# Attention and gated layer in one kernel: scores moved behind the AV of the quad before, and each output tile written by one DMA instead of four

## Chip, cores, metric

One core of one Trainium2 chip. The metric is the device time of one execution in microseconds. Times differ from run to run by about 1%, so each ratio uses runs made in the same rounds on the same chip. The span that a profile shows is 1.5 to 2 us shorter than the device time of the same run.

## The reference, cut to what matters

```python
# 8 batches, 8 heads, 512 local + 32 global tokens, head_dim 64, window 32
out_g = softmax(scale * q_g @ k_all.T) @ v_all                 # global tokens see all
s_ll  = where(|i - j| <= 32, scale * q_l @ k_l.T, -1e9)        # local ones: a band ...
s_lg  = scale * q_l @ k_g.T                                    # ... and the global tokens
out_l = softmax(concat([s_lg, s_ll])) @ concat([v_g, v_l])
x = concat([out_g, out_l], axis=2).transpose(0, 2, 1, 3).reshape(4352, 512)
h = x @ w_in                                                   # 512 x 2048
out = (h * sigmoid(1.702 * h)) @ w_out                         # 2048 x 512, out is float32
```

## The kernel before

The work is cut into 16 quads (a quad is four heads of one batch). In the steady part, phase `i` holds the hidden layer of batch `i`, its four output tiles of 128 tokens, and between them the two quads of batch `i+1`. In the traces TensorE's work stands in the order of the program (in the prediction's lines of one quad: scores at 219.11 us, then 220.19, 220.50 and 221.56). AV is the product of the attention weights with the values. Two kinds of PSUM space matter: the score tile `s4` of four banks, and four single banks that rotate through the pool `psP` and serve everything else: `op` (an output tile), `kb` (products with the global keys), three `ov` and one `og` (AV of the local and the global tokens), `hp` (a piece of the hidden layer).

```python
psS = ctx.enter_context(tc.tile_pool(name="psS", bufs=1, space=bass.MemoryType.PSUM))
psP = ctx.enter_context(tc.tile_pool(name="psP", bufs=4, space=bass.MemoryType.PSUM))
...
keep(17, psP.tile([128, 512], F32, name="w", tag="p"))     # dummy matmuls of 512 columns
...
# S: scores of local q and k; its first round ends with the small product gk (q_g, k_g)
# K: local q with k_g into a bank kb; XK: exp of kb -> ek
# ekU(unit): first matmul group of one ov bank, from ek (unit 0: sums, 1 and 2: values)
# U(unit): the banded part added to the same ov;  Gm: og, the global tokens' output
# R, XL, G: VectorE's normalisation (R transposes ov of unit 0: sT)
def ekUs(self, nxt=None):
    if nxt:
        nxt.K(0)
    self.ekU(0)
    if nxt:
        nxt.K(1)
    self.ekU(1)
    self.ekU(2)

def UG(self, nxt=None):
    self.ekUs(nxt)
    for unit in range(3):
        self.U(unit)
    self.Gm()
...
def o_out(i, tci, op):                      # one output tile: 128 tokens x 512
    ob = moe.tile([128, d_model], F32, name="ob", bufs=6)
    nc.scalar.activation(ob, op, AF.Copy, scale=0.5)
    if i < B:
        rows = out[i * S + Sg : (i + 1) * S, :].rearrange("(r t) m -> t r m", t=16)
        for j in range(4):                  # token = 16 r + t: 32 rows, 32 KB apart
            nc.sync.dma_start(out=rows[4 * tci + j], in_=ob[32 * j : 32 * j + 32, :])
    else:
        ...                                 # global tokens: 32 rows of batch 4*tci + j
...
def phase_o(i):
    ...
    o(0)
    c.S(0)          # scores of the next quad
    a.UG(c)         # AV of this quad, with K of the next
    a.RXG()
    c.XK()
    ...
```

The softmax here doesn't subtract the row's maximum and nothing guards it: scores larger than these inputs give would overflow.

Of the kernel before, what the change touches and what calls it, by code (L numbers as in the profile page):

```python
# [20 lines left out]
def kernel(  # L21
# [137 lines left out]

    def keep(n, ps):  # L160
        for _ in range(n):
            nc.tensor.matmul(ps, lhsT=warm[:, 0:128], rhs=warm, start=True, stop=True)

    keep(17, psP.tile([128, 512], F32, name="w", tag="p"))

# [41 lines left out]
    kgT = consts.tile([128, NQ, 32], F32)  # L207
    def transpose_g(lo, hi):
        for dst, s in ((kgT, rkg), (qgT, rqg)):
            nc.vector.transpose(dst[:, lo:hi, :32], s[:, lo:hi].bitcast(F32))  # L210
# [24 lines left out]
    class Quad:  # L235
        def __init__(self, Q):
# [10 lines left out]
            self.E = [None, None]  # L247
            self.st = {}

        def Tk(self, cs=(0, 1, 2, 3)):  # L250
# [14 lines left out]

        def ext(self):
            for (r0, nr), t0, n in zip(WIN, (0, 20, 1, 20), (4, 3, 3, 4)):
                nc.vector.tensor_copy(
                    self.qt[:, t0 : t0 + n, r0 : r0 + nr],
                    qgT[:, self.Q, : n * nr].rearrange("p (t r) -> p t r", t=n))  # L270

        def S(self, rnd, split=False, warm=0):
            if split:
                ps = [pbank("s") for _ in range(4)]
                keep(warm, ps[0])
            else:
                pt = psS.tile([128, 4, 512], F32, name="s4")
                ps = [pt[:, j, :] for j in range(4)]
            off = 0
            for c in (2 * rnd, 2 * rnd + 1):  # L280
# [11 lines left out]
                off += n * nr  # L292
            if rnd == 0:
                self.gk(ps[2][:, RW : RW + 32], self.qg)
# [14 lines left out]
        def X(self, rnd):  # L309
            e = self.E[rnd]  # L310
            if isinstance(self.ps, list):
                for j in range(4):
                    nc.scalar.activation(e[:, j, :RW], self.ps[j][:, :RW], AF.Exp, scale=scale)
                return
            nc.scalar.activation(e[:, :, :RW], self.ps[:, :, :RW], AF.Exp, scale=scale)  # L315
            if rnd == 0:
                nc.scalar.activation(e[:, 2, RW:], self.ps[:, 2, RW : RW + 32], AF.Exp, scale=scale)  # L317
# [12 lines left out]
        def eg(self):  # L330
            self.egb = att.tile([128, 4, 32], BF16, name="eg")
            nc.vector.tensor_mul(
                self.egb, bd,
                self.E[0][:, 2, RW:].rearrange("p (o w) -> p o w", o=1).to_broadcast([128, 4, 32]))

# [14 lines left out]
        def ekUs(self, nxt=None):  # L350
            if nxt:
                nxt.K(0)
            self.ekU(0)
# [58 lines left out]
        def UG(self, nxt=None):  # L412
            self.ekUs(nxt)
            for unit in range(3):
                self.U(unit)
            self.Gm()
# [46 lines left out]
    def o_out(i, tci, op):  # L463
        ob = moe.tile([128, d_model], F32, name="ob", bufs=6)
        nc.scalar.activation(ob, op, AF.Copy, scale=0.5)  # L465
        if i < B:
            rows = out[i * S + Sg : (i + 1) * S, :].rearrange("(r t) m -> t r m", t=16)
            for j in range(4):
                nc.sync.dma_start(out=rows[4 * tci + j], in_=ob[32 * j : 32 * j + 32, :])
        else:  # L470
            for j in range(4):
                r = (4 * tci + j) * S
                nc.sync.dma_start(out=out[r : r + Sg, :], in_=ob[32 * j : 32 * j + 32, :])

# [16 lines left out]
    make_mask()  # L491
    cast_g32(0, "qk")
    transpose_g(0, 2)
    a.ext()
    a.Tq(0, 8)
    a.Tq(8, 16)
    a.Tk((0, 1))
    a.Tk((2, 3))
    load_rest()
    a.S(0)  # L500
# [8 lines left out]
    a.M(0)  # L509
    c.Tq()  # L510
    c.S(0)
    c.X(0)
    a.M(1)
    load_g32(1, "qkv", hold=True)
    a.eg()
    a.ekUs(c)
    c.XK()
# [10 lines left out]
    a.XL(1)  # L528
    c.eg()
    gTs[0] = moe.tile([128, FC, TB], BF16, name="gT")  # L530
    pt = pts[0] = psS.tile([128, 4, 512], F32, name="s4")
    c.ekUs()
    for unit in range(3):
        c.U(unit)
    c.R()
    for fc in range(4):
        h_mm(0, fc, pt[:, fc, :], (0, 1))
# [37 lines left out]
    osteps(0, (0, 1), (0, 0), (1, 1), (1, 0))  # L575
    c.ext()
    a.S(0)
    a.K()
    a.X(0)
# [7 lines left out]
    a.M(1)  # L587
    osteps(0, (1, 2), (1, 3))
    c.S(0)
    c.X(0)  # L590
    c.M(0)
    c.eg()
    osteps(0, (2, 0), (2, 1), (2, 2), (2, 3))
    c.S(1)
    c.X(1)
    a.ekUs(c)
    c.XK()
    for unit in range(3):
        a.U(unit)
    a.Gm()  # L600
    a.R()
    c.M(1)
    a.XL(0)
    a.XL(1)
    a.G()
    osteps(0, (3, 0), (3, 1))
    c.UG()
# [9 lines left out]
    for fc in range(FC):  # L617
        h_step(1, fc)
        if fc == 3:
            a.S(0)  # L620
            a.K()
            a.X(0)
            a.XK()
        if fc == 5:
# [4 lines left out]
    def phase_o(i):  # L629
# [15 lines left out]
        a.M(1)  # L645
        o(0)
        c.S(0)
        a.UG(c)
        a.RXG()
# [12 lines left out]
        if n < B:  # L662
            o(2)
            a2.S(0)
            c.UG(a2)
        else:
            for f4 in range(3):
                o_mm(i, 8 + f4)
            c.ekUs()
            for unit in range(3):  # L670
                c.U(unit)
            o_mm(i, 11)
            c.Gm()
# [18 lines left out]
    for st in range(FC):  # L692
        h_step(B, st)
        o_mm(B - 1, st)
    for st in range(FC // 2):
        o_mm(B, st)


# [28 lines left out]
```

## Time and profile before

| | before |
|---|---|
| median of device times | 318.1 us (316.8 to 320.3, 4 runs) |
| profiled span | 317.3 us |
| start, up to the first scores of phase 1 | 76.45 us |
| eleven quads, from there to the last scores | 183.5 us, 34.63 us per batch |
| from there to the start of the last activation | 52.4 us |
| tail, from the start of the last activation to the end | 5.0 us |

The prediction below shows the main lines of this profile. Three more from its page are the granted clock in forty slices, the queue of the hardware-issued DMAs (packets, MB, share of the time of 16 engines) and the output DMAs (count, size of one, time from issue to landing in us).

```profile
PEclk9989999999999999999999999999999999999998
...
q1 hardware_dynamic: 7904, 9.25, 11.7%
...
out_dram<-ob SPq DMA_DIRECT2D x136, 64.0 KB, 1.8
```

Taken one by one from the trace, its 4352 packets of 2 KB, all of the output, last 0.124 us in the mean.

### The profile page before, as it was taken

The numbers are of one execution on the slowest core, as the hardware profiler recorded it, in microseconds if no ns is written. First come the engines' busy times: TensorE is split into PE (matmuls) and PEld (weight loads), VectorE is DVE, ScalarE is ACT, GpSimd is POOL, SyncE is SP. The second block draws the span as 40 slices with busy tenths as digits, with TensorE's granted clock in tenths as the row PEclk, the third lists the DMA queues.
The fourth block names the chain that finished last, engine by engine and source line by source line (L and its number), as shares of the span: only waits on it lengthen the run. The fifth ranks groups of instructions, "written<-read, shape, count | busy, mean of one in ns | idle before, by whom it ended". The sixth has DMA issues, their size and how long they took to land.

```text
span 317.3 us, 7687 instructions
## 1 busy us (share of the span) xinstructions
PE 301.0 (95%) x3154; PEld 145.6 (46%) x3189; DVE 211.0 (66%) x462; ACT 165.8 (52%) x253; POOL 79.9 (25%) x131
## 2 busy tenths in 40 slices
PE   8759999999999999999999999999999998999993
PEld 2334444444554454544554455445454454445651
DVE  7766864879667767787866866786767855583310
ACT  4714765277355663565536736466346551673420
POOL 8911578686118000720036000300000000000000
PEclk9989999999999999999999999999999999999998
DMA  8999999999929411990259312901120012101122
GB/s 156 143 188 206 206 136 176 164 164 119 137 53 176 74 34 36 115 151 2 55 71 158 56 35 52 118 0 28 40 52 20 0 43 61 33 2 33 33 68 67
DMA packets 59907, 27.44 MB, mean 86 GB/s; under 512 B 43232, under 2 KB 51424, under 8 KB 59872
## 3 DMA queue, kind: packets, MB, share of 16 engines
q0 software_dynamic: 51536, 17.11, 50.0%
q1 hardware_dynamic: 7904, 9.25, 11.7%
q10 hardware_dynamic: 432, 0.59, 0.6%
q8 instruction: 25, 0.41, 0.5%
q14 instruction: 10, 0.08, 0.1%
HBM read 35.13 MB, written 8.91 MB: 139 GB/s over the span
## 4 chain that ended last, share of the span: by engine, by line
PE 72%; DMA 13%; POOL 6%; DVE 4%; issue 2%; ACT 1%; POOLq 0%; ACTq 0%
PE op L458 33%; PE hp L433 30%; DMA w_out_sb<-in_moe_w_out_dram 9%; PE s L286 4%; POOL rk L84 3%; DMA rq<-in_q_l_dram 3%; DVE sT L391 3%; POOL v L97 2%; PE ov L347 2%; PE ov L368 2%; DMA v<-in_v_l_dram 1%; POOL w_in_sb L217 1%; DVE gT L441 1%; ACT th L440 1%; PE s L305 0%
## 5 line engine op out<-in xcount | busy, mean ns | idle before, releaser
L458 PE MATMUL op<-w_out_sb,gT 128*128 128x512 bf16 x519 | 123.2, 379 | 2.9 <-DVE xL L400 0.8
L441 DVE SCALAR_TENSOR_TENSOR gT<-th,hp 128x512 bf16<-128x512 f32 (+1 forms) x140 | 91.1, 657 | 42.3 <-ACT th L440 41.6
L433 PE MATMUL hp<-xL,w_in_sb 128*128 128x512 bf16 x487 | 108.2, 379 | 0.6
L440 ACT ACTIVATE th<-hp 128x512 f32<-128x512 f32 (+1 forms) x140 | 80.0, 573 | 43.1 <-PE hp L433 40.5
L433 PEld LDWEIGHTS <-w_in_sb 128*128 128x128 bf16 x576 | 56.4, 98 | 65.5 <-issue 2.2
L458 PEld LDWEIGHTS <-gT 128*128 128x128 bf16 x544 | 51.7, 98 | 59.0 <-issue 4.1
L465 ACT ACTIVATE ob<-op 128x512 f32<-128x512 f32 x34 | 20.3, 597 | 77.6 <-PE op L458 77.5
L315 ACT ACTIVATE e<-s 128x1712 bf16<-128x1712 f32 x31 | 49.4, 1595 | 5.9 <-PE s L305 5.4
L97 POOL DMA_DIRECT2D v<-in_v_l_dram x36 | 26.9, 754 | 97.8 <-PE og L385 90.7
L84 POOL DMA_DIRECT2D rk<-in_k_l_dram x64 | 34.9, 554 | 16.1 <-DMA w_in_sb<-in_moe_w_in_dram 7.0
L391 DVE STREAM_TRANSPOSE sT<-ov 128x512 f32<-128x512 f32 x16 | 11.5, 717 | 36.2 <-PE ov L368 36.2
L322 DVE TENSOR_TENSOR e<-e,mask 128x1408 bf16<-128x1408 bf16 x32 | 27.9, 873 | 7.6 <-ACT e L315 7.3
L286 PE MATMUL s<-q,kT 32*128 32x200 bf16 (+1 forms) x512 | 21.3, 284 | 1.3 <-ACT e L317 0.7
L400 DVE TENSOR_TENSOR xL<-ov,rs 128x512 bf16<-128x512 f32 x32 | 20.7, 686 | 1.5
L286 PEld LDWEIGHTS <-kT 32*128 32x128 bf16 x512 | 11.0, 95 | 15.4 <-issue 10.4
L338 ACT ACTIVATE ek<-kb 128x512 bf16<-128x512 f32 x16 | 9.6, 602 | 7.0 <-PE kb L305 7.0
L368 PE MATMUL ov<-e,v 128*32 128x192 bf16 (+1 forms) x512 | 13.2, 246 | 0.0
L347 PE MATMUL ov<-ek,rvg 32*32 32x512 bf16 x128 | 10.0, 375 | 1.9 <-DVE xL L400 1.9
L395 DVE STREAM_TRANSPOSE rs<-rT 128x512 f32<-128x512 f32 x16 | 11.4, 711 | 0.6
L256 DVE STREAM_TRANSPOSE kT<-rk 128x512 f32<-128x512 f32 (+1 forms) x17 | 11.3, 670 | 0.0
L259 DVE STREAM_TRANSPOSE q<-rq 128x512 f32<-128x512 f32 (+1 forms) x17 | 10.8, 643 | 0.0
L368 PEld LDWEIGHTS <-v 128*32 128x32 bf16 x512 | 10.6, 100 | 0.2 <-issue 0.2
(64 smaller groups left out, 145.1 us busy)
## 6 DMA issues: line engine op xcount, KB each, us to landing
out_dram<-ob SPq DMA_DIRECT2D x136, 64.0 KB, 1.8
rk<-in_k_l_dram POOLq DMA_DIRECT2D x64, 64.0 KB, 4.2
v<-in_v_l_dram POOLq DMA_DIRECT2D x28, 128.0 KB, 4.6
rq<-in_q_l_dram POOLq DMA_DIRECT2D x6, 512.0 KB, 6.4
w_in_sb<-in_moe_w_in_dram POOLq DMA_DIRECT2D x4, 512.0 KB, 13.1
w_out_sb<-in_moe_w_out_dram POOLq DMA_DIRECT2D x4, 512.0 KB, 14.0
rq<-in_q_l_dram POOLq DMA_DIRECT2D x3, 256.0 KB, 7.8
q<-in_q_l_dram ACTq DMA_DIRECT2D x1, 512.0 KB, 4.1
```

The source lines that it names most:

```text
L84: nc.gpsimd.dma_start(out=loaded[b][0][32 * j : 32 * j + 32, u], in_=kf[b, j][:, u])
L97: nc.gpsimd.dma_start(out=vtiles[b % 2][p, s, :, :, :D], in_=vf[b, t][:, hs])
L286: nc.tensor.matmul(ps[j][:, off : off + n * nr], lhsT=self.k[p, 128 * c : 128 * c + 128, e], rhs=self.q[p, t0 : t0 + n, r0 : r0 + nr, e], ...
L315: nc.scalar.activation(e[:, :, :RW], self.ps[:, :, :RW], AF.Exp, scale=scale)
L322: nc.vector.tensor_mul(e, e, mask[:, rnd : rnd + 1, :].to_broadcast([128, 4, LW]))
L368: nc.tensor.matmul(ov[32 * j : 32 * j + 32, :].rearrange("p (t r) -> p t r", t=16)[:, :, r0 : r0 + nr], lhsT=lv, rhs=self.E[c // 2][:, j, ...
L391: nc.vector.transpose(sT.rearrange("p a b -> p (a b)"), self.st[0])
L400: nc.vector.tensor_mul(self.x[:, 2 * self.u + h, :], self.st[1 + h], self.st["rs"])
L433: nc.tensor.matmul(hp[:, : width(i)], lhsT=w_in_c[:, fc // 8, kc, fc % 8 // 2, :, fc % 2], rhs=(xL[i] if i < B else xG)[:, kc, :], start=( ...
L440: nc.scalar.activation(th[:, :n], hp[:, :n], AF.Tanh, scale=0.851)
L441: nc.vector.scalar_tensor_tensor(gTs[i][:, fc, :n], in0=th[:, :n], scalar=1.0, in1=hp[:, :n], op0=ALU.add, op1=ALU.mult)
L458: nc.tensor.matmul(op, lhsT=gTs[i][:, fc, tci * 128 : tci * 128 + 128], rhs=w_out_sb[:, fc, :], start=(first and fc == 4 * f4), stop=(fc = ...
```

## The change

Its intent: (1) the scores of the next quad follow the AV of this one, so that VectorE's transpose `sT` is done when the next output tile needs its bank; (2) one DMA per output tile, the last tile in two halves; (3) in batches 0 and 1 and in the last quad the AV goes unit by unit; (4) finer dummies, with q made ready before k at the start. The core of it:

```diff
-    keep(17, psP.tile([128, 512], F32, name="w", tag="p"))
+    keep(62, psP.tile([128, 512], F32, name="w", tag="p"), 128)
...
+        def gg(self):                       # gk ahead, opens the score tile
+            self.pt = psS.tile([128, 4, 512], F32, name="s4")
+            self.gk(self.pt[:, 2, RW : RW + 32], self.qg)
...
         def ekUs(self, nxt=None):
             if nxt:
+                nxt.gg()
                 nxt.K(0)
             self.ekU(0)
...
-            rows = out[i * S + Sg : (i + 1) * S, :].rearrange("(r t) m -> t r m", t=16)
-            for j in range(4):
-                nc.sync.dma_start(out=rows[4 * tci + j], in_=ob[32 * j : 32 * j + 32, :])
+                rows = out[i * S + Sg : (i + 1) * S, :].rearrange("(r t) m -> t r m", t=16)[4 * tci : 4 * tci + 4]
+            ...                             # global tokens: [4 * tci : 4 * tci + 4, :Sg]
+            nc.sync.dma_start(out=rows[:, :, lo:hi], in_=ob[:, lo:hi])
...
         o(0)
-        c.S(0)
         a.UG(c)
+        c.S(0)
         a.RXG()
...
             o(2)
-            a2.S(0)
             c.UG(a2)
+            a2.S(0)
         else:
             for f4 in range(3):
                 o_mm(i, 8 + f4)
-            c.ekUs()
             for unit in range(3):
+                c.ekU(unit)
                 c.U(unit)
...                                          # start: order of casts, AV of quads 0 to 3
-    for st in range(FC // 2):
+    for st in range(4):
         o_mm(B, st)
+    o_out(B, 1, None)                        # last tile: two halves of 256 columns
```

More of the change, by code (lines that the diff above doesn't have):

```diff
@@ L158, with keep @@
     nc.vector.memset(warm, 0.0)
-    def keep(n, ps):
+    def keep(n, ps, w=512):
         for _ in range(n):
-            nc.tensor.matmul(ps, lhsT=warm[:, 0:128], rhs=warm, start=True, stop=True)
-    keep(17, psP.tile([128, 512], F32, name="w", tag="p"))
+            nc.tensor.matmul(ps[:, :w], lhsT=warm[:, 0:128], rhs=warm[:, :w], start=True, stop=True)
+    keep(62, psP.tile([128, 512], F32, name="w", tag="p"), 128)
     qtiles = []
@@ L207, with transpose_g @@
     kgT = consts.tile([128, NQ, 32], F32)
-    def transpose_g(lo, hi):
-        for dst, s in ((kgT, rkg), (qgT, rqg)):
+    def transpose_g(lo, hi, names="qk"):
+        for name, dst, s in (("q", qgT, rqg), ("k", kgT, rkg)):
+            if name not in names:
+                continue
             nc.vector.transpose(dst[:, lo:hi, :32], s[:, lo:hi].bitcast(F32))
@@ L248, in __init__ @@
             self.st = {}
+            self.pt = None
+            self.gr = 0
         def Tk(self, cs=(0, 1, 2, 3)):
@@ L264, in T, with ext @@
             self.Tq()
-        def ext(self):
-            for (r0, nr), t0, n in zip(WIN, (0, 20, 1, 20), (4, 3, 3, 4)):
+        def ext(self, cs=(0, 1, 2, 3)):
+            for c in cs:
+                (r0, nr), t0, n = WIN[c], (0, 20, 1, 20)[c], (4, 3, 3, 4)[c]
                 nc.vector.tensor_copy(
@@ L276, in S @@
             else:
-                pt = psS.tile([128, 4, 512], F32, name="s4")
+                pt = self.pt if rnd == 0 and self.pt is not None else psS.tile([128, 4, 512], F32, name="s4")
                 ps = [pt[:, j, :] for j in range(4)]
@@ L292, in S @@
                 off += n * nr
-            if rnd == 0:
+            if split:
+                self.gr = rnd
                 self.gk(ps[2][:, RW : RW + 32], self.qg)
@@ L312, in X @@
                 for j in range(4):
-                    nc.scalar.activation(e[:, j, :RW], self.ps[j][:, :RW], AF.Exp, scale=scale)
+                    n = RW + 32 if j == 2 else RW
+                    nc.scalar.activation(e[:, j, :n], self.ps[j][:, :n], AF.Exp, scale=scale)
                 return
             nc.scalar.activation(e[:, :, :RW], self.ps[:, :, :RW], AF.Exp, scale=scale)
-            if rnd == 0:
+            if rnd == 0 and self.pt is not None:
                 nc.scalar.activation(e[:, 2, RW:], self.ps[:, 2, RW : RW + 32], AF.Exp, scale=scale)
@@ L333, in eg @@
                 self.egb, bd,
-                self.E[0][:, 2, RW:].rearrange("p (o w) -> p o w", o=1).to_broadcast([128, 4, 32]))
+                self.E[self.gr][:, 2, RW:].rearrange("p (o w) -> p o w", o=1).to_broadcast([128, 4, 32]))
+        def gg(self):
+            self.pt = psS.tile([128, 4, 512], F32, name="s4")
+            self.gk(self.pt[:, 2, RW : RW + 32], self.qg)
         def XK(self):
@@ L412, in UG @@
         def UG(self, nxt=None):
-            self.ekUs(nxt)
+            if nxt:
+                self.ekUs(nxt)
             for unit in range(3):
+                if not nxt:
+                    self.ekU(unit)
                 self.U(unit)
@@ L464, in o_out @@
         ob = moe.tile([128, d_model], F32, name="ob", bufs=6)
-        nc.scalar.activation(ob, op, AF.Copy, scale=0.5)
-        if i < B:
-            rows = out[i * S + Sg : (i + 1) * S, :].rearrange("(r t) m -> t r m", t=16)
-            for j in range(4):
-                nc.sync.dma_start(out=rows[4 * tci + j], in_=ob[32 * j : 32 * j + 32, :])
-        else:
-            for j in range(4):
-                r = (4 * tci + j) * S
-                nc.sync.dma_start(out=out[r : r + Sg, :], in_=ob[32 * j : 32 * j + 32, :])
+        last = i == B and tci == B // 4 - 1
+        for lo, hi in ((0, 256), (256, 512)) if last else ((0, 512),):
+            if last:
+                op = pbank("op")
+                for fc in range(FC):
+                    nc.tensor.matmul(op[:, lo:hi], lhsT=gTs[i][:, fc, tci * 128 : tci * 128 + 128],
+                                     rhs=w_out_sb[:, fc, lo:hi], start=(fc == 0), stop=(fc == FC - 1))
+            nc.scalar.activation(ob[:, lo:hi], op[:, lo:hi], AF.Copy, scale=0.5)
+            if i < B:
+                rows = out[i * S + Sg : (i + 1) * S, :].rearrange("(r t) m -> t r m", t=16)[4 * tci : 4 * tci + 4]
+            else:
+                rows = out.rearrange("(b s) m -> b s m", b=B)[4 * tci : 4 * tci + 4, :Sg]
+            nc.sync.dma_start(out=rows[:, :, lo:hi], in_=ob[:, lo:hi])
     def act4(i, hf):
@@ L491 @@
     make_mask()
-    cast_g32(0, "qk")
-    transpose_g(0, 2)
-    a.ext()
+    cast_g32(0, "q")
+    transpose_g(0, 2, "q")
+    a.ext((0, 1))
     a.Tq(0, 8)
@@ L497 @@
     a.Tk((0, 1))
+    a.ext((2, 3))
     a.Tk((2, 3))
+    cast_g32(0, "k")
+    transpose_g(0, 2, "k")
     load_rest()
@@ L510 @@
     c.Tq()
+    c.gg()
     c.S(0)
@@ L515 @@
     a.eg()
-    a.ekUs(c)
+    c.K(0)
+    a.ekU(0)
+    c.K(1)
+    a.ekU(1)
+    a.ekU(2)
     c.XK()
@@ L528 @@
     a.XL(1)
-    c.eg()
     gTs[0] = moe.tile([128, FC, TB], BF16, name="gT")
     pt = pts[0] = psS.tile([128, 4, 512], F32, name="s4")
-    c.ekUs()
     for unit in range(3):
+        c.ekU(unit)
         c.U(unit)
     c.R()
+    c.eg()
     for fc in range(4):
@@ L576 @@
     c.ext()
+    a.gg()
+    a.K()
     a.S(0)
-    a.K()
     a.X(0)
@@ L588 @@
     osteps(0, (1, 2), (1, 3))
+    a.ekUs(c)
     c.S(0)
+    c.XK()
     c.X(0)
-    c.M(0)
-    c.eg()
-    osteps(0, (2, 0), (2, 1), (2, 2), (2, 3))
-    c.S(1)
-    c.X(1)
-    a.ekUs(c)
-    c.XK()
-    for unit in range(3):
-        a.U(unit)
+    a.U(0)
+    a.R()
+    osteps(0, (2, 0), (2, 1))
+    a.U(1)
+    a.U(2)
+    c.S(1)
     a.Gm()
-    a.R()
-    c.M(1)
     a.XL(0)
@@ L605 @@
     a.G()
-    osteps(0, (3, 0), (3, 1))
+    c.M(0)
+    c.eg()
+    c.X(1)
+    c.M(1)
+    osteps(0, (2, 2), (2, 3), (3, 0), (3, 1))
     c.UG()
@@ L619 @@
         if fc == 3:
+            a.gg()
+            a.K()
             a.S(0)
-            a.K()
+            a.XK()
             a.X(0)
-            a.XK()
         if fc == 5:
@@ L646, in phase_o @@
         o(0)
+        a.UG(c)
         c.S(0)
-        a.UG(c)
         a.RXG()
@@ L663, in phase_o @@
             o(2)
+            c.UG(a2)
             a2.S(0)
-            c.UG(a2)
         else:
@@ L668, in phase_o @@
                 o_mm(i, 8 + f4)
-            c.ekUs()
             for unit in range(3):
+                c.ekU(unit)
                 c.U(unit)
```

## The prediction

> **What bounds the kernel now.** I read the page first, for the shares of the engines, then the timeline of one quad in the steady part, then the chain of work and the timeline of the start, then the tail.
>
> ```profile
> PE 301.0 (95%) x3154; PEld 145.6 (46%) x3189; DVE 211.0 (66%) x462; ACT 165.8 (52%) x253; POOL 79.9 (25%) x131
> ...
> DMA  8999999999929411990259312901120012101122
> ```
>
> TensorE is at 95%; no other engine is near. DMA is full for the first eleven of the forty slices, to about 87 us, and has room afterwards. So there are two regimes. After about 61 us the order of TensorE's work sets the time; before it the loads do, as the chain of work says (start, duration, what):
>
> ```profile
> 13.15 18.19 DMA w_out_sb<-in_moe_w_out_dram
> 31.34 0.28 issue
> 31.63 9.87 DMA w_out_sb<-in_moe_w_out_dram
> 41.49 0.28 issue
> ...
> 49.86 8.61 DMA rq<-in_q_l_dram
> 58.47 0.28 issue
> ```
>
> **Steady part.** From 97.3 us on every batch takes 34.62 or 34.63 us: hidden layer 13.8, four output tiles of about 3.55, and two quads of attention. The timeline of one quad (start, duration, line, operation), where a 3.5 us output tile ends just before 219.1:
>
> ```profile
> 219.11 0.66 PE L286 MATMUL s<-q,kT 32*128 32x200 bf16 x16
> 219.21 0.60 ACT L465 ACTIVATE ob<-op 128x512 f32<-128x512 f32 x1 [1.95 <-PE op L458]
> ...
> 220.19 0.38 PE L347 MATMUL ov<-ek,rvg 32*32 32x512 bf16 x4
> ...
> 220.50 0.49 PE L368 MATMUL ov<-e,ones 128*32 128x160 bf16 x16
> ...
> 221.04 0.72 DVE L391 STREAM_TRANSPOSE sT<-ov 128x512 f32<-128x512 f32 x1 [2.31 <-PE ov L368]
> ...
> 221.56 0.21 PE L385 MATMUL og<-rvg,eg 128*32 128x66 bf16 x4
> ...
> 221.81 3.61 PE L458 MATMUL op<-w_out_sb,gT 128*128 128x512 bf16 x15
> ```
>
> The output tile at 221.81 takes the PSUM bank that sT reads until 221.76, so it starts 0.24 us after the last og matmul. Where nothing is awaited (start of the hidden layer at 27.3 us) the same step is 0.12 us. The change goes after this wait: 0.12 us per quad.
>
> **Start.** Three things stand in it. First the busy times of one window (PE, PEld, DVE, ACT, POOL, then granted clock, DMA share, GB/s), then the timeline.
>
> ```profile
> 20.97:24.38 3.41, 2.81 (x39) 1.75 (x40) 2.60 (x5) 0.00 (x0) 1.08 (x2) 0.50 1.14 205
> ```
>
> ```profile
> 21.24 0.32 PE L368 MATMUL ov<-e,ones 128*32 128x160 bf16 x3 [1.51 <-issue]
> ...
> 23.07 4.06 PE L433 MATMUL s<-xL,w_in_sb 128*128 128x512 bf16 x15 [0.33 <-issue]
> ```
>
> TensorE stands 1.51 us in the middle of the AV of quad 1 with no semaphore to wait for; the first 16 KB packet of the instruction queue began at 18.72 us, late. Before it, two rv matmuls each waited about 1 us for XL to free a bank. Then 3.41 us run at half clock (the 0.50). The hidden layer so starts at 23.07, although the first quarter of w_in landed at 20.83.
>
> **What the Trainium skill says.** (1) TensorEngine Tiling (Array Packing), Key Properties: "Changing tiling mode (not just tile) drains the TensorE". The trace agrees: the start-to-start step at a change of tile shape exceeds the streaming time by 0.09 to 0.12 us. (2) Runtime: NRT & Kernel Launch, Instruction fetch mechanics: instructions come in blocks of 256 (16 KB) by a DMA queue. The trace shows 25 packets of 16384 B and the stall after 449 recorded PE instructions, plausible as number 512 with the preamble. (3) TensorE: Matmul & The Clock Gate, part 1: the clock halves after a little-used, free-running window of 3.4 us. The trace has exactly one such window inside the kernel. (4) DMA: Bandwidth & Descriptors, Why a DMA increments its semaphore by 16: a DMA uses the largest number of engines up to 16 that divides the slowest dimension of both sides. Nothing in this trace tests it: all output DMAs have 32 rows outermost.
>
> **The change, part by part.**
>
> *Scores after AV (steady).* Take the last output matmul at 0. Before: S at +0.31, the K and ek matmuls from +0.91, the last ek group at +1.39, U at +1.70, og at +2.63 (last +2.77), next output tile at +3.01. Afterwards the tiny gg takes the place at +0.31, K follows at +0.38, and the last ek group would come at +0.80. But its bank is that of the output tile just ended: only four banks rotate, the other three hold kb and the first two ov. ScalarE evicts that tile from +0.415 for 0.597, so to +1.01, and 0.053 more passes (as from sT's end to the output tile): +1.065. Before, at +1.39, this wait was hidden. So U +1.38, og +2.31 to +2.45, S at +2.57 (0.03 streaming, 0.10 drain), 0.39 within S and 0.21 to the output tile: +3.17. That is 0.16 us worse, not 0.12 better: it removes 0.12 of waiting for sT and uncovers 0.27 of waiting for the eviction. Eleven quads of batches 2 to 7 have this form: **+1.75 us**. The number of shape changes per quad stays at four.
>
> *Last quad, unit by unit.* sT starts some 0.44 us earlier, since its first U follows its own ek. Before, the last output tile of that phase waited 0.99 us after og, for XL. Four more shape changes lie inside this wait: **-0.44 us**.
>
> *Start.* With q cast and transposed first and gk moved to the second round, S(0) comes about 0.6 us earlier (0.3 of k cast, 0.17 transpose, 0.19 of two copies); X loses one small act. 62 dummies of 128 columns end some 0.3 to 0.6 us earlier than 17 of 512. U(0) of quad 1 no longer waits for three ek groups. I carry this on: quad 1 done near 19 us, no long hole. The 45 extra dummies are 90 instructions, so block borders move 90 instructions forward: the fetch is asked for near 8 us, before w_in is queued, and the stall probably goes. But w_in lands at 20.83, 23.06, 25.91 and 28.82. First eight matmuls from 20.9, next eight from 23.1 to 24.8, steps 4 to 7 to 28.3, steps 8 to 15 at 0.86 each from 28.8: end near 35.5 against 37.7. A half-clock window there would take back one of the **-2.2 us**. In the output steps of batch 0 w_out's quarters (31.3, 33.8, 38.9, 41.5) and q of quad 3 (44.07) then take up part of it, and AV before S with output steps between gives some back: waits of 0.59, 0.39 and 0.21 us at 54 to 59 us go. I arrive at hidden layer 1 at about 58.4 instead of 60.94: **-2.4 us**.
>
> *One DMA per output tile.* Four issues of 0.32 to 0.43 us become one, which no one waits for except at the end. But the output view is now 4 x 32 x 512, outermost 4, so by (4) it would run on 4 engines. An estimate from that page's 27 GiB/s: 32 packets of 2 KB at 0.07 us, 2.3 us on each of four engines instead of 0.6 on sixteen. While DMA is full, every tile so puts the loads back by up to 1.7 us. Up to three tiles fall before rq of batch 2 (landing 58.47) and rkg and rqg (58.9, 59.8): they would land near 62 to 64.5. VectorE, in order, has T of quad 4 before the first gT of hidden layer 1; TensorE fills four banks and stands to about 66.8, against 65.69 before. So this part alone would turn the start from -2.4 to about **+0.5** (from -1 to +2).
>
> *Tail.* Before, ScalarE ends at 312.94, four issues follow to 314.69, the last lands at 315.99, and the epilogue ends at 317.3.
>
> ```profile
> 309.51 5.18 SPq L473 DMA_DIRECT2D out_dram<-ob  x8
> 312.34 0.60 ACT L465 ACTIVATE ob<-op 128x512 f32<-128x512 f32 x1 [2.86 <-PE op L458]
> ```
>
> Halves of 256 columns take TensorE the same time (0.109 us a matmul in the last hidden layer), the act 0.38 instead of 0.60, one issue instead of four. On 16 engines the last would land at about 314.7: -1.3. On 4 engines the previous tile and the first half still occupy them: landing 315.5 to 316.5, about +0.
>
> *Sum.* On 4 engines: +1.75 -0.44 +0.5 +0 = +1.8. On 16: +1.75 -0.44 -2.4 -1.3 = -2.4.
>
> **Rivals.** *A: reordering as intended.* The eviction is quicker than I think or the bank another one; then each quad gains 0.11 us, 1.2 in all, and with 16 engines the total is 318.6 -1.2 -0.4 -2.4 -1.3 = 313.3. For it: the change is plainly made to hide sT. Against: the arithmetic of four banks. *B: the DMA of four engines becomes the bound*, in the start and where loads fill DMA again (131.95 to 145.7 us: share 0.99); if loads came 8 us late, 324. Against: later loads have a batch of slack. *C: the start is hidden behind loads anyway*: only steady and tail count, about 319.5 to 320. For it: the chain of work is DMA up to 58 us.
>
> **Range and chances.** I weigh 4 engines at 0.75: 0.75 x 1.8 - 0.25 x 2.4 = +0.75. That the change is the work of somebody who was looking for time speaks for rival A; I take 0.9 off. So 318.5 us. The runs before spread by 3.5 us, one clock window's worth; the range is 314.5 to 322.5. Two per cent is 6.4 us, which no sum above reaches except rival B at its worst. Faster 0.05, same 0.90, slower 0.05.
>
> **What would show it.** Steady: the last ek group waits for the act of the output tile, the batch takes 34.95 us instead of 34.63; rival A: 34.4. Start: no 1.5 us hole, hidden layer 0 starts by 21 us and ends near 35.5. Output DMA: a landing of over 3 us where DMA is idle, against 1.6 before, says four engines; hidden layer 1 stops after four steps until rq lands. Tail: landing 3.4 us or more after the last act, or 2. A batch of under 34.5 us, or output landing in under 2 us, makes the prediction wrong.

## The result, and the profile after

The kernel after takes 328.5 us in the median (327.2 to 330.2, 4 runs); the ratio is 1.032, 95% interval 1.024 to 1.040: slower, where the prediction had 318.5 us (314.5 to 322.5). Ratios here are the mean time of one kernel's fast runs over the mean of the other's fast runs of the same rounds, so they are not quite the ratio of the medians that are quoted. The profiled run of after took 330.2 us and that of before 319.1 us, so the two traces differ by the same 11.1 us as the runs. They can be cut at four events that both have:

| stretch (us) | before | after | difference | predicted |
|---|---|---|---|---|
| start, to the first S of phase 1 | 76.45 | 83.73 | **+7.28** | +0.5 |
| eleven quads, to the last S | 183.53 | 185.49 | **+1.96** | +1.75 |
| to the start of the last activation | 52.36 | 52.00 | **-0.36** | -0.44 |
| tail, to the end of the span | 5.00 | 7.23 | **+2.23** | 0 |
| span | 317.35 | 328.45 | **+11.1** | +1.8 |

Two of the four terms are as predicted. The two others are those with the output DMA in them. From the page of after, the rows of TensorE, of its clock and of the DMA engines by fortieths, the queue and the output DMAs:

```profile
PE   7779999559999999999999999999999999999991
...
PEclk9999999959999999999999999999999999999997
DMA  8999996999948901393129701900121011101222
...
q1 hardware_dynamic: 5996, 9.24, 10.5%
...
out_dram<-ob SPq DMA_DIRECT2D x33, 256.0 KB
```

TensorE's row has a dip of two slices (57 to 74 us) that before does not have, and the clock row has a 5 there. The DMA row has a 6 in its seventh slice, from 49 us on, where before it was full. So DMA engines were idle just before TensorE stood still for want of data.

**The start.** The chain of work of after, from 46 to 69 us (start, duration, what):

```profile
46.02 10.70 DMA rk<-in_k_l_dram
...
57.78 10.55 DMA rqg<-in_q_g_dram
...
68.35 0.24 DVE qgT L212
```

Before, the chain ended its DMA part with rq at 58.47. Now it goes on to 68.33 through rqg, the small load of global q for batch 2. The timeline of after shows what TensorE does meanwhile:

```profile
58.03 3.62 PE L448 MATMUL hp<-xL,w_in_sb 128*128 128x512 bf16 x16
...
64.50 0.71 DVE L263 STREAM_TRANSPOSE q<-rq 128x512 f32<-128x512 f32 x1 [4.76 <-DMA rq<-in_q_l_dram]
...
68.35 0.24 DVE L212 STREAM_TRANSPOSE qgT<-rqg 128x64 f32<-128x64 f32 x1 [3.14 <-DMA rqg<-in_q_g_dram]
...
68.78 0.24 PE L311 MATMUL s<-qgT,kgT 32*32 32x32 bf16 x8 [7.13 <-DVE kgT L212]
...
71.55 0.61 PE L448 MATMUL hp<-xL,w_in_sb 128*128 128x512 bf16 x1
```

Hidden layer 1 begins at 58.03, 2.91 us earlier than before (60.94). After its first four steps (16 matmuls) TensorE stands 7.13 us, until VectorE has transposed rqg. Two windows of after, and one of before for comparison (stretch, length, then PE, PEld, DVE, ACT, POOL busy, granted clock, DMA share, GB/s; the share is the summed time of packets over the time of 16 engines, so it can pass 1 where packets overlap):

```profile
50.00:54.00 4.00, 3.84 (x46) 1.81 (x40) 2.88 (x7) 2.19 (x2) 1.08 (x2) 1.00 0.63 108
...
64.80:75.06 10.26, 5.34 (x40) 2.03 (x42) 4.33 (x12) 3.97 (x6) 7.13 (x12) 0.50 1.00 99
```

```profile
50.00:54.00 4.00, 3.67 (x90) 1.92 (x89) 1.28 (x4) 2.67 (x3) 3.31 (x5) 1.00 1.13 180
```

The clock stays at half for three windows of 3.41 us, from 64.8 to 75.06, of which the last 6.28 us hold work. The start adds up: hidden layer 1 to the first S of phase 1 took 15.51 us before and 25.70 after, 10.19 more; 7.13 is the stop, and the 3.06 left is half of the 6.28 us at half clock, within a tenth. With the 2.91 us gained ahead of it, this gives +7.28.

Why did rqg land at 68.33 instead of 59.77? From 50 to 54 us the DMA share is 0.63 in after and 1.13 in before, and POOL, which issues the loads, is busy 1.08 us instead of 3.31. POOL begins to issue the v loads at the same time in both (41.66 and 41.77), but the one issued at 43.57 in after landed at 52.09, that of 43.67 in before at 46.66. POOL issued five of the next eight k loads and then stood for 4.19 us, until that v had landed; so the rest went out late: rq at 55.75 instead of 49.86, rqg at 57.78 instead of 51.50. What had been put among the v loads are the DMAs of the first two output tiles, issued at 43.10 and about 45.5. The lines of after:

```profile
43.10 10.34 SPq L492 DMA_DIRECT2D out_dram<-ob  x3
...
45.48 2.70 POOL L84 DMA_DIRECT2D rk<-in_k_l_dram  x5
...
52.37 1.08 POOL L84 DMA_DIRECT2D rk<-in_k_l_dram  x2 [4.19 <-DMA v<-in_v_l_dram]
...
55.75 0.71 POOL L88 DMA_DIRECT2D rq<-in_q_l_dram  x1 [0.60 <-DMA rk<-in_k_l_dram]
```

And those of before, where POOL issues its k loads without a stop:

```profile
45.20 10.47 SPq L469 DMA_DIRECT2D out_dram<-ob  x12
...
45.58 4.30 POOL L84 DMA_DIRECT2D rk<-in_k_l_dram  x8
...
49.86 0.71 POOL L88 DMA_DIRECT2D rq<-in_q_l_dram  x1
```

The reader sees only a wait for a small load; the cause is two transfers of output three steps earlier (a_one_t23 below shows it).

**One quad in the steady part.** The timeline of after, to be set against the lines from 219.11 us on in the prediction; the output tile's last matmul began at 87.575:

```profile
87.99 0.60 ACT L487 ACTIVATE ob<-op 128x512 f32<-128x512 f32 x1 [1.95 <-PE op L473]
...
88.64 0.40 PE L358 MATMUL ov<-ek,rvg 32*32 32x512 bf16 x4
...
90.16 0.67 PE L291 MATMUL s<-q,kT 32*128 32x200 bf16 x16
...
90.76 1.47 PE L473 MATMUL op<-w_out_sb,gT 128*128 128x512 bf16 x5
```

ScalarE evicts the output tile until 88.59, and 0.05 us later the third ek group starts: it waits for that bank. From the last matmul of one output tile to the first of the next are 90.758 - 87.575 = 3.18 us; before it was 3.01.

**The tail.** After, timeline:

```profile
318.35 3.82 SPq L492 DMA_DIRECT2D out_dram<-ob  x3
...
321.22 0.38 ACT L487 ACTIVATE ob<-op 128x256 f32<-128x256 f32 x1 [1.36 <-PE op L485]
```

One issue instead of four follows the last activation (321.63, against 312.97 to 314.27 before), but the last packet ends 5.35 us after the activation does (326.95), against 2.70 us before (315.64).

**The output DMA by itself.** In the trace each output DMA of after comes with four 4-byte packets besides its data; before, each of the four came with 16, and in the experiments a_8eng and a_16eng it is 8 and 16. So these packets count the engines. Where nothing else is under way, a tile's data take 4.4 us from the first packet to the end of the last in after. With one DMA on 8 and on 16 engines (experiments below) it is 2.5 and 1.3 us, and as four DMAs of 16 engines, before, 1.85 us. The mean time of a 2 KB packet in the first three is 0.128, 0.137 and 0.125 us, so about 16 GB/s.

### The profile page after: what moved, and what is told of

It is laid out like the page before. It is cut to its first block, busy times and chain, and to the rows that moved or that the text cites. A ratio compares the mean times of both kernels' runs of the same rounds, so it can differ in the third digit from the quotient of the medians.

```text
span 328.5 us, 7682 instructions
## 1 busy us (share of the span) xinstructions
PE 303.9 (93%) x3215; PEld 150.4 (46%) x3250; DVE 211.5 (64%) x462; ACT 167.7 (51%) x253; POOL 80.1 (24%) x131
## 4 chain that ended last, share of the span: by engine, by line
PE 74%; DMA 15%; POOL 5%; ACT 2%; issue 1%; DVE 0%; POOLq 0%
PE hp L448 31%; PE op L473 31%; DMA w_out_sb<-in_moe_w_out_dram 8%; PE s L291 4%; PE ov L380 4%; DMA rk<-in_k_l_dram 3%; DMA rqg<-in_q_g_dram 3%; ACT ob L487 2%; POOL v L97 2%; PE ov L358 2%; POOL rk L84 2%; PE op L485 1%; POOL w_in_sb L219 1%; PE og L397 1%; PE kb L311 0%
## 5 line engine op out<-in xcount | busy, mean ns | idle before, releaser
L473 PE MATMUL op<-w_out_sb,gT 128*128 128x512 bf16 x504 | 120.1, 380 | 2.3 <-DMA w_out_sb<-in_moe_w_out_dram 0.8
L448 PE MATMUL hp<-xL,w_in_sb 128*128 128x512 bf16 x487 | 109.6, 383 | 0.6 <-issue 0.2
L473 PEld LDWEIGHTS <-gT 128*128 128x128 bf16 x528 | 49.2, 98 | 59.1 <-issue 6.9
L487 ACT ACTIVATE ob<-op 128x512 f32<-128x512 f32 (+1 forms) x35 | 20.5, 585 | 63.3 <-PE op L473 60.8
L358 PE MATMUL ov<-ek,rvg 32*32 32x512 bf16 x128 | 12.4, 380 | 0.8
L311 PE MATMUL kb<-q,kgT 32*32 32x512 bf16 x128 | 10.4, 399 | 1.2 <-DVE gT L456 0.7
L380 PEld LDWEIGHTS <-v 128*32 128x32 bf16 x512 | 9.8, 96 | 2.6 <-issue 2.3
```

The source lines that it names most:

```text
L380: nc.tensor.matmul(ov[32 * j : 32 * j + 32, :].rearrange("p (t r) -> p t r", t=16)[:, :, r0 : r0 + nr], lhsT=lv, rhs=self.E[c // 2][:, j, ...
L448: nc.tensor.matmul(hp[:, : width(i)], lhsT=w_in_c[:, fc // 8, kc, fc % 8 // 2, :, fc % 2], rhs=(xL[i] if i < B else xG)[:, kc, :], start=( ...
L473: nc.tensor.matmul(op, lhsT=gTs[i][:, fc, tci * 128 : tci * 128 + 128], rhs=w_out_sb[:, fc, :], start=(first and fc == 4 * f4), stop=(fc = ...
L487: nc.scalar.activation(ob[:, lo:hi], op[:, lo:hi], AF.Copy, scale=0.5)
```

## The experiments

Twelve kernels were run, each beside the kernel before in the same rounds. All twelve gave the correct result. "First S" is the first S of phase 1, the end of the start; "tail" goes from the end of the last activation to the end of the span.

| kernel | median us (runs) | ratio to before, 95% | batch | first S | rqg landed | tail |
|---|---|---|---|---|---|---|
| before | 317.3 | | 34.63 | 76.45 | 59.77 | 4.41 |
| after | 328.5 (4) | 1.032, 1.024 to 1.040 | 34.98 | 83.73 | 68.33 | 6.85 |
| a_16eng | 317.5 (12) | 1.001, 0.999 to 1.003 | 35.05 | 75.33 | 62.07 | 4.09 |
| a_8eng | 317.8 (20) | 1.002, 1.000 to 1.004 | 34.99 | 73.53 | 60.28 | 4.12 |
| a_fourdma | 316.7 (20) | 0.998, 0.996 to 1.000 | 34.98 | 72.06 | 57.48 | 4.44 |
| b_onedma | 323.7 (4) | 1.018, 1.013 to 1.023 | 34.63 | 77.89 | 64.63 | 7.11 |
| a_one_late | 319.6 (4) | 1.008, 1.006 to 1.011 | 34.98 | 73.44 | 57.06 | 6.59 |
| a_one_t23 | 319.4 (20) | 1.006, 1.004 to 1.008 | 34.98 | 73.72 | 56.97 | 6.96 |
| b_order | 319.4 (22) | 1.006, 1.004 to 1.008 | 34.98 | 74.33 | 57.79 | 4.40 |
| b_dummies | 316.6 (12) | 0.997, 0.995 to 1.000 | 34.63 | 74.52 | 59.60 | 4.40 |
| a_four_17 | 316.7 (20) | 0.998, 0.996 to 1.000 | 34.98 | 73.02 | 59.77 | 4.44 |
| a_four_sback | 316.0 (22) | 0.995, 0.993 to 0.998 | 34.88 | 72.53 | 58.56 | 4.45 |
| a_four_kb | 314.1 (6) | 0.990, 0.986 to 0.994 | 34.42 | 72.27 | 58.32 | 4.44 |
| a_four_kb_g8 | 313.6 (4) | 0.989, 0.987 to 0.992 | 34.42 | 72.95 | 57.27 | 3.87 |

Names with a_ start from the kernel after, those with b_ from before. The columns to the right of the ratio come from one trace each; "first S" moves by one to three microseconds with the landing of the loads, and small differences in it mean nothing. The median of before is that of the experiments' rounds.

The theory: the four engines of the output DMA cause the loss. The rivals: one DMA of 256 KB is bad as such, whatever the number of engines; or the new order of the start is.

### The number of engines: a_16eng, a_8eng, a_fourdma

a_16eng keeps one DMA per tile and gives the tile every fourth column of gT. These columns are ordered with `t` outermost, 32 `r` each, so the tile's output becomes 16 x 8 rows (all `t`, every fourth `r`) instead of 4 x 32, and the DMA can use 16 engines. The two global tiles become 8 x 16 rows, for 8 engines:

```diff
-    lhsT=gTs[i][:, fc, tci * 128 : tci * 128 + 128]
+    lhsT=gTs[i][:, fc, tci : width(i) : width(i) // 128]
-    rows = ... .rearrange("(r t) m -> t r m", t=16)[4 * tci : 4 * tci + 4]     # 4 x 32 x 512
+    rows = ... .rearrange("(r t) m -> t r m", t=16)[:, tci::4]                  # 16 x 8 x 512
-    rows = out.rearrange("(b s) m -> b s m", b=B)[4 * tci : 4 * tci + 4, :Sg]   # global
+    rows = out.rearrange("(b s) m -> b s m", b=B)[:, tci:Sg:2]                  # 8 x 16 x 512
```

> The changed kernel, still one DMA per output tile, but each tile takes every fourth token, so that the output view is 16 x 8 rows (8 x 16 for the two global tiles) and the DMA can use 16 (8) engines instead of 4. Theory (four engines): loads of batch 2 land as in the kernel before (rqg near 60 us instead of 68), hidden layer 1, started near 58, does not stop for 7 us, no window at half clock follows, the last landing comes some 2.5 us after the last act instead of 5.7. Start 10 us and tail 3 us better than the changed kernel: about 315 us. Rival (the new order itself makes the loads late or TensorE stop): no more than the tail changes, 325 us or more.

Measured: 317.5 us, 11.0 us less than after. TensorE's wait for the transposes of rqg and rkg in hidden layer 1 shrinks from 7.13 to 0.36 us (a wait of 0.75 us for VectorE's gT follows, as one of 0.73 us did in after), the clock is not halved there, the tail is 4.09 us. The hoped-for 315 was missed: the batch takes 35.05 us, and the loads still landed somewhat later (rqg at 62.07).

a_8eng takes every second column of one half of gT, 8 x 16 rows, so that 8 engines can be used:

```diff
-    lhsT=gTs[i][:, fc, tci * 128 : tci * 128 + 128]
+    lhsT=gTs[i][:, fc, tci // 2 * 256 + tci % 2 : tci // 2 * 256 + 256 : 2]
-    rows = ... .rearrange("(r t) m -> t r m", t=16)[4 * tci : 4 * tci + 4]
+    rows = ... .rearrange("(r t) m -> t r m", t=16)[8 * (tci // 2) : 8 * (tci // 2) + 8, tci % 2 :: 2]
```

> The changed kernel with one DMA per tile that has 8 x 16 rows, thus 8 engines. Theory (each 2 KB packet holds its engine 0.127 us): a tile alone takes 2.0 us of packets instead of 4.06, half of the harm at the start is left: rqg lands between 60 and 65 us, TensorE stops for 0 to 3 us; total 317 to 320. Rival (a single DMA of 256 KB is the trouble, whatever the engines): near 326.

Measured: 317.8 us, within what was expected. No wait for rqg is left, and one of 0.52 us for gT. Half of the harm at the start was expected to stay; less does (first S at 73.53 us, against 72.06 in a_fourdma below and 83.73 in after). Half the engines are enough.

a_fourdma puts the four DMAs back and leaves all else of the change:

```diff
-            nc.sync.dma_start(out=rows[:, :, lo:hi], in_=ob[:, lo:hi])
+            for j in range(4):
+                nc.sync.dma_start(out=rows[j][:, lo:hi], in_=ob[32 * j : 32 * j + 32, lo:hi])
```

> The changed kernel with the four DMAs of 32 rows per tile of before (also for both halves of the last tile). Theory (four engines): start as in a_16eng, hidden layer 1 runs through from 58 us; tail about as the kernel before, since four issues follow the last act again: about 316.5 us. Rival (order): 325 us or more.

Measured: 316.7 us, 0.998 of before. Its timeline has no stop:

```profile
56.84 3.62 PE L448 MATMUL hp<-xL,w_in_sb 128*128 128x512 bf16 x16
...
60.38 0.22 PE L311 MATMUL s<-qgT,kgT 32*32 32x32 bf16 x8
...
61.59 10.54 PE L448 MATMUL hp<-xL,w_in_sb 128*128 128x512 bf16 x48
```

The three together rule out both rivals as causes by themselves: the same 256 KB in one DMA on 8 or 16 engines costs about 1 us at most (317.8 and 317.5 against 316.7), and all of the change without the one DMA is no slower than before. In the changed kernel the DMA on four engines is worth 328.5 - 316.7 = 11.8 us, give or take the difference of about 1 us between the rounds.

### The DMA alone: b_onedma

The kernel before with one DMA per tile:

```diff
-            rows = ... ; for j in range(4): nc.sync.dma_start(out=rows[4 * tci + j], ...)
+            rows = ...[4 * tci : 4 * tci + 4]
+            nc.sync.dma_start(out=rows, in_=ob)
```

> The kernel before with nothing but one DMA of 4 x 32 x 512 per output tile. Theory (four engines): rqg lands near 68 instead of 59.8, hidden layer 1 stops for about 5 us, perhaps a half-clock window after it, tail 2 us longer: about 326 us. Rival (order of the change is the cause): 318 to 320 us, the tail alone.

Measured: 323.7 us over four runs, 323.2 over the three fast ones; the ratio, 1.018 (1.013 to 1.023), leaves open whether the loss reaches 2%. The tail grew by 2.7 us, as expected. The rest is a miss: rqg landed at 64.63 and not near 68, hidden layer 1 waits 0.33 us and not 5, no window at half clock follows it, and first S comes 1.4 us later. So there is a loss without the reorder, but of 6 us and not 11, and it does not have the stop that makes up most of the loss in after. That stop takes both: the DMA on four engines and the changed start. (Tail and first S make 4.1 of the 6 us. The trace of before is of a run 1.8 us over the median of before, which may be the rest.)

In b_onedma rqg landed 4.9 us later than in before, in after 8.6. The first tile is issued at 45.48 there, 2.4 us later than in after. Its packets begin at 47.24 us, when five of the six v loads have landed; in after they begin at 44.98, before any of them has. So the changed start brings the tiles forward into the v loads. Since the two kernels differ in more than this, it is not shown that this alone makes the difference.

### Where in the kernel: a_one_late, a_one_t23

Four DMAs for batch 0 only, one on four engines for all later tiles:

```diff
+            if i == 0:
+                for j in range(4):
+                    nc.sync.dma_start(out=rows[j], in_=ob[32 * j : 32 * j + 32, :])
+            else:
+                nc.sync.dma_start(out=rows[:, :, lo:hi], in_=ob[:, lo:hi])
```

> The changed kernel with four DMAs per tile for batch 0 alone; all later tiles by one DMA on 4 engines. Theory (the 4-engine DMA hurts where loads fill DMA and TensorE soon needs them, so only by the tiles of batch 0, and at the very end): start as a_fourdma (first S of phase 1 near 72 us), batches of 34.98, only the tail some 2.5 us longer than a_fourdma: about 319 us. Rival (every 4-engine tile costs something): 322 us or more.

Measured: 319.6 us, as expected. Going back to four DMAs for four tiles out of 34 wins 8.9 of the 11.8 us; of the 2.9 left, 2.15 are in the tail (6.59 against 4.44), and the rest is no more than noise. Then only the first two tiles are written by four DMAs (`if i == 0 and tci < 2`):

> a_one_late with only tiles 0 and 1 of batch 0 by four DMAs; tiles 2 and 3 of batch 0 and all later ones by one DMA on 4 engines. What is open: the 4-engine tiles set the start back by much more in the changed kernel (rqg 68.3 us) than in b_onedma (64.6). Theory: the first two tiles meet the v loads of quad 3, whose 128-byte packets alternate with 2 KB packets on the four engines; with these two away rqg lands by 62 us and the total is 320 to 321. Rival (every tile before rqg has the same share): half of the harm stays, rqg near 63 to 64, total 323 to 324.

Measured: 319.4 us, rqg at 56.97. So tiles 0 and 1 of batch 0, issued while the v and k loads of the next batches fill the DMA engines, do all of the harm at the start. The 28 local tiles after batch 0 do none that shows: the batch takes 34.98 us as in a_fourdma. The loads then have slack.

### The steady part: b_order, a_four_sback, a_four_kb

b_order is the kernel before with only the order in the steady part changed (`c.gg(); a.UG(c); c.S(0)` in place of `c.S(0); a.UG(c)`):

> The kernel before with AV ahead of S in the steady part alone. Theory: the batch goes from 34.63 to 35.0 us, total 2 us more than the kernel before, 319.2. Rival (intent of the change): the batch goes to 34.4, total 316.

Measured: 319.4 us and 34.98 us per batch, as expected. The order costs 0.35 us per batch, 0.18 per quad, on its own.

a_four_sback is a_fourdma with the order of the steady part turned back (`gg`, S, then UG):

> a_fourdma with S ahead of AV again in the steady part, all else as changed. Theory (the order costs 0.18 us a quad): a batch takes 34.63 us, total 2 us less than a_fourdma, 314.7. Rival (the longer batch comes of something else in the change): a batch stays at 35.

Measured: 34.88 instead of the expected 34.63. This is a miss, and the fault of the edit: `gg` now stands ahead of S as a group of its own shape, one more change of shape in each quad. Two quads of 0.125 us would explain it (34.63 + 0.25), and 0.09 to 0.12 us is what the prediction read for such a change; no run isolates it. It is no clean undo; b_order is the better test.

a_four_kb takes away what the third ek group waits for. K of the next quad goes into the fourth bank of the score tile that `gg` has opened, and its exp comes before S overwrites it. So one fewer of the four rotating banks is used per quad, and the bank of the output tile just ended is asked for one step later:

```diff
-                self.kb = pbank("kb")
+                self.kb = self.pt[:, 3, :] if in_s else pbank("kb")
...
-                nxt.K(0)
+                nxt.K(0, in_s=True)
...
             self.ekU(1)
+            if nxt:
+                nxt.XK()
             self.ekU(2)
```

> a_fourdma with K of the next quad in bank 3 of the score tile (its exp emitted before S), in the quads where AV comes before S, so that ov of the last ek group gets a free bank instead of that of the output tile just ended. Theory (eviction of the output tile stands on TensorE's path, some 0.25 us a quad; with it away the reorder brings its 0.11): a batch takes 34.4 us instead of 34.98, 11 quads x 0.29 = 3.2 us, total about 313.5. Rival (the quad is longer for its changes of tile shape, whatever bank is used): a batch stays at 35, total 316.7.

Measured: 34.42 us per batch and 314.1 us, as expected. Its timeline:

```profile
110.95 0.60 ACT L489 ACTIVATE ob<-op 128x512 f32<-128x512 f32 x1 [1.94 <-PE op L475]
...
111.32 0.39 PE L358 MATMUL ov<-ek,rvg 32*32 32x512 bf16 x4
111.64 0.49 PE L382 MATMUL ov<-e,ones 128*32 128x160 bf16 x16
...
112.83 0.66 PE L291 MATMUL s<-q,kT 32*128 32x200 bf16 x16
113.43 0.82 PE L475 MATMUL op<-w_out_sb,gT 128*128 128x512 bf16 x3
```

The last ek group (111.32) no longer waits for the activation that ends at 111.55, and the step from one output tile to the next is 113.428 - 110.534 = 2.89 us: 0.12 under before, the 0.12 that the change was after.

### The dummies: b_dummies, a_four_17

The kernel before with 62 dummies of 128 columns, and a_fourdma with 17 of 512 (`keep(17, ...)`):

> The kernel before with only the 62 dummies of 128 columns. Theory (instruction fetch): the 90 added instructions bring the fetch of the third block forward, the 1.5 us hole in the AV of quad 1 near 19.5 us goes or moves, the hidden layer starts near 21 instead of 23; since loads of batch 2 still bound the start, the total is 316.5 to 318. Rival (the hole has to do with the loads of w_in or with the AV of quad 1 itself): the hole stays where it is, 318.

> a_fourdma with the 17 dummies of 512 columns again, 90 instructions fewer. Theory (instruction fetch): the first packet of the instruction queue begins near 18 to 19 us instead of 11, TensorE stands 1 to 1.5 us with nothing to wait for around the 449th recorded PE instruction (AV of quad 1), and hidden layer 0 starts later; total 0.5 to 1.5 us over a_fourdma. Rival (the fetch comes late only with the long dummies' own timing, or was chance): no hole.

Measured: b_dummies 316.6 us, 0.997, its hole of 1.5 us is gone and hidden layer 0 starts at 21.19 us, as expected; a_four_17 316.7 us, as a_fourdma, and without a hole: a miss. The first packet of the instruction queue comes 10.2 to 11.8 us in for every kernel with 62 dummies, and 16.8 to 19.1 us in for every one with 17: that part of the theory holds in all fourteen traces. But the hole did not come back in a_four_17 (packet at 16.77), nor is it in b_order (17.03); it shows only in before and b_onedma, with 18.72 and 19.11. So the hole goes with the two latest packets; that late fetching causes it, and what else it takes, is not shown. The effect on the time is under 1 us.

### The best of it: a_four_kb_g8

a_four_kb with the two tiles of global tokens, the last two of the kernel, by one DMA on 8 engines, for a shorter tail:

```diff
-        lhsT=gTs[i][:, fc, tci * 128 : tci * 128 + 128]
+        lhsT=... if i < B else gTs[i][:, fc, tci : 256 : 2]
-            rows = out.rearrange("(b s) m -> b s m", b=B)[4 * tci : 4 * tci + 4, :Sg]
+            rows = out.rearrange("(b s) m -> b s m", b=B)[:, tci:Sg:2]
```

> a_four_kb with the two global tiles by one DMA on 8 engines (every second token), for the tail: one issue instead of four after the last act. Theory: last act's end to the end of the span 3.8 to 4.1 us instead of 4.4; total 0.4 us less than a_four_kb, 313.7, the best of all. Rival: the tail is bound by the landing itself, same as a_four_kb.

Measured: 313.6 us, 0.989 of before, tail 3.87 against 4.44. It is the fastest kernel; its lead over a_four_kb is within the noise.

## Why the prediction was wrong, and where right

**Steady part, right.** Predicted +1.75 us, measured +1.96; batch predicted 34.95, measured 34.98. The mechanism, the last ek group waiting for the eviction of the output tile that has just ended, is seen in the trace, comes alone with b_order and goes with a_four_kb. The last quad: -0.44 predicted, -0.36 measured.

**Start without the DMA, right as far as it can be read.** Hidden layer 1 at 58.03 us, predicted 58.4; hidden layer 0 first at 19.78, "by 21"; its end at 34.8, "near 35.5"; no 1.5 us hole.

**One DMA per output tile, the failed step.** The prediction had the main steps of the mechanism: "so by (4) it would run on 4 engines", "TensorE fills four banks and stands to about 66.8". What failed is the size, at four points, and a link that no term had: POOL's wait.

- "32 packets of 2 KB at 0.07 us, 2.3 us on each of four engines". Measured: 0.13 us a packet and 4.4 us a tile. The estimate took 27 GiB/s from the Trainium skill, DMA: Bandwidth & Descriptors, Specifications, though the page of before gave 15.6 GB/s in its line of the queue, shown above. A measured figure was to be had and a stated one was used.
- "every tile so puts the loads back by up to 1.7 us", "they would land near 62 to 64.5". Measured: rq at 64.48, rqg at 68.33. The delay was reckoned as the extra time of the four engines. It is larger: a v load alone came 5.4 us late, and POOL stood 4.19 us until it had landed, so that the later loads were not even issued and other DMA engines had no work (DMA share 0.63 where before had 1.13). The earlier start (-2.4) and the DMA (+2.9) were added as if independent. In the traces the DMA puts first S back by 1.44 us in the old start (b_onedma against before) and by 11.67 in the new one (after against a_fourdma; one trace each), where the first tile comes forward to 43.10 us, into the v loads.
- The stop cost more than its length: the half clock added 3.06 us to the 7.13. The prediction reckoned with a half-clock window in hidden layer 0 but not here.
- The tail: "+0" on four engines. Measured +2.23. The three last DMAs (512 KB on four engines, issued from 318.35 on) are not done until 326.95. An estimate with the measured packet, 64 x 0.13 = 8.3 us on each engine from 318.35 on, gives 326.7.

The start term so came out at +7.28 against +0.5 (the prediction's own 66.8 against 65.69 would be +1.1). Rival B ("the DMA of four engines becomes the bound", "if loads came 8 us late, 324") was the right one and was given too little: rqg came 8.6 us late. Its argument against, "later loads have a batch of slack", is right, as a_one_late shows, but the harm is done before there is slack.

**The weighing, wrong too.** Four engines were weighed at 0.75 and 0.9 us taken off because the change's author was looking for time. The rule for the number of engines fits every run here; the size was the open part, and there the chance of a larger delay was worth more than 0.05. The prediction also says that rival B at its worst reaches two per cent, 6.4 us; its own 324 is only 5.4 us above 318.6.

**What stays open.** That tiles 0 and 1 of batch 0 do the harm is shown. How they hold back the v loads is only argued: the tile's 2 KB packets and the 128-byte ones of v would take turns on the four engines, and a v load would be done only when its share there is. The packets, counted one by one in the traces, fit this: in before the 128-byte packets of these v loads are over at 47.95 us; in after 342 of them still begin between 49 and 53 us, beside 103 of 2 KB of the output, and the last at 53.88. But the traces do not say on which engine a packet runs, and no run tested it. Nor is it shown why POOL's k loads wait for a v load, or why rqg came 8.6 us late in after and only 4.9 in b_onedma, beyond the tiles' position relative to the v loads.

## What to carry to other kernels

Before four DMAs are merged into one, look at the outermost dimension of what is written: 4 there meant 4 engines, and a single tile then took 4.4 us in place of 1.85 (four DMAs) or 1.3 (one on 16 engines); a tile that takes every second or fourth token makes it 8 or 16. Take the rate of a packet from the queue's own line of the profile, and treat a transfer that sits on a few engines as a delay of the loads beside it (here 5.4 us on one of v), first of all while the loads are the bound. Do not add up two parts of a change before asking what the one moves into the other: here the DMA alone cost first S 1.4 us, and 11.7 together with the earlier start. In a reorder on TensorE follow each bank to its last reader: the wait that was hidden before may be the next one in line, and a bank elsewhere, here one of the score tile, can take it away.

## What the Trainium skill lacked or had wrong

- DMA: Bandwidth & Descriptors, Specifications: about 27 GiB/s per engine. For the output writes of 2 KB packets the runs show 15.6 GB/s (before) and 0.125 to 0.137 us a packet on 4, 8 and 16 engines, about 16 GB/s. Its rule for the number of engines (Why a DMA increments its semaphore by 16) holds: 4.4, 2.5 and 1.3 us a tile for outermost dimensions of 4, 8 and 16.
- None of the pages gives the cost of a transfer confined to a few engines for loads spread over all of them: in after v landed at 52.09 instead of 46.66 us, DMA share 0.63 instead of 1.13, TensorE standing 7.13 us.
- TensorE: Matmul & The Clock Gate, part 1, has the clock halve after an idle window of about 3.4 us and puts the cost at the throttled time times (1 - K/N). In after the stop of 7.13 us gave three windows at half clock, 10.24 us, which makes an estimate of 5.12 us by that page; the runs show 3.06, since TensorE had work in only 6.28 us of them. And in before the window ahead of the half clock, 17.56 to 20.97 us, was not idle: TensorE was busy in 1.17 of its 3.41 us.
- Runtime: NRT & Kernel Launch, Instruction fetch mechanics, calls the cost of a block's fetch mostly hidden. With DMA full, the first packet of the instruction queue came at 16.8 to 19.1 us with 17 dummies, and TensorE stood 1.5 us in the two traces where it was latest (18.72 and 19.11).
- TensorEngine Tiling (Array Packing), Key Properties, gives no figure for the drain: 0.09 to 0.12 us in before; one change more per quad in a_four_sback goes with 0.125 us.
